# Agent attention and a top-1 expert layer on one core: the agents' scale in four parts, first queries and next keys at other steps, stores and transposes asked for later

## The chip, the cores and the metric

The kernel runs on one core of one Trainium2 chip. A time is device microseconds (us) of one execution of the whole program. The kernel before has a median of 1130.12 us over three runs (1129.23 to 1131.7). The engines are called as the profile calls them: PE is the matrix engine (PEld its weight loads), DVE the vector engine, ACT the scalar engine, POOL the general one, SP the engine that issues most transfers.

## The reference

Four batches of 11,456 tokens with 128 channels pass through attention by way of 49 agents, and the result through a layer of 8 experts of which each token uses the best one.

```python
scale = 1 / sqrt(128)
def sm(a, b):                       # softmax of scale * a b^T over the last axis
    ...
a2k = sm(agents, k)                 # (4, 49, 11456)
agent_v = a2k @ v                   # (4, 49, 128)
x = (sm(q, agents) @ agent_v).reshape(45824, 128)
logits = x @ w_gate                 # 8 experts
expert_idx = argmax(logits)
gate_w = softmax(logits)[expert_idx]
for e in range(8):
    xe = x[expert_idx == e]
    out[expert_idx == e] = gate_w * (relu(xe @ w1[e]) @ w2[e])
```

The inputs q, k and agents are drawn with a standard deviation of 0.8, v with 0.1.

## The kernel before

**Tiling.** A batch is cut into 11 chunks of 1024 tokens and one of 192. A chunk of keys or queries is loaded (`load`, L306), its scale is found (squares on ACT, L359; the power of two from bits of the sum on DVE and POOL, L230 to L237), and it is split into two float16 parts, high by ACT (L393) and low by DVE (L395), in the tile `hl`. A transfer that transposes (`turn_over`, L421) writes `hT`, in which the channels lie on the partitions; there are two buffers of it for keys and two for queries. Scores against the agents are three matmuls for each 128 tokens (`scores`, L462 to L464). From scores of keys come exponentials S and their two parts `eh`: ACT L537 and L562, POOL L556 (a running sum `es`) and L564. They are multiplied with the values (`values`, L594, accumulated by DVE L603). From scores of queries come exponentials E and `mm`, which a transfer transposes to `M` (L716).

**The loop.** The product of attention with the chosen expert's first matrix is folded into 49 rows `Ah`, `Al`, so a batch's main loop is 23 groups of 512 tokens times 8 slices of 128 hidden channels, 184 steps. A step is layer 1 of its slice (PE L1300 and L1301 into `ph`, of which there are four), relu and splitting (ACT L1306, DVE L1307 into `hh`), and layer 2 of the slice five steps back (12 matmuls, L1321). Each batch uses one expert in the loop (the commonest); tokens that chose another are gathered behind all four loops and done in blocks. Step 7 of batch 1 is written b1:7 here. By layer 1's first matmul, b0:0 starts 71.9 us into the profiled execution, b1:0 at 340.4, b2:0 at 593.0, b3:0 at 832.7, and the last step at 1069.9.

**What sets the order.** All other work is laid between the steps by a table of numbers. `at(t, f)` puts a piece of work f at step t, counted over all four batches, on a heap; `after(dt, f)` puts it dt steps behind the piece that is running. The pieces are issued in order of t. On each engine the program order is that of the issue, and the engine keeps to it, whatever is ready. SP's own order is kept too (`issue_after(queue[-1])`). In `attention`, KS and KT are the step of a batch's first keys, counted from the batch's own step 0, and the steps between chunks; QA, QB and QC the same for queries. A later batch's keys and values, and its first queries, therefore lie in the loops ahead of its own: KS = -211 is step 157 of the batch two ahead; the agents' scale (`agent_squares`, `agent_split`) stands three and two steps ahead of the first keys, so that of batch 2 at b0:154 and that of batch 3 at b1:154. DTR, DTE, DEX and DST are how many steps behind its producer a transfer or an addition is put: the transposes of `hl` to `hT` (DTR), the transposes of mm (DTE), the store of exponentials (DEX), and the stores of the output (DST). For the first batch everything ahead of step 0 is a prologue with numbers of its own (KS0 and so on).

Of the kernel before, what the change touches and what calls it, by code (L numbers as in the profile page):

```python
# [12 lines left out]
F32 = mybir.dt.float32  # L13
# [3 lines left out]
AF = mybir.ActivationFunctionType  # L17
# [4 lines left out]
P = 128  # L22
A = 49
# [22 lines left out]
KS0, KT0, KL0, VT0, VL0, QS0, QT0, QL0 = -200, 2, 4, 2, 1, -172, 3, 2.5  # L46
VE, T1, TF0, TF1, TL, TLM, Q0 = 12, 1.75, 3, 1.5, 18, 10, 2

KS, KT, VT, VL, VL4, TW0, TW1, DW = -211, 9, 5.3, 8, 5, 8, 2.5, 1
QA, QB, QC, QB3, KL, LL, UD, RG, D1, DL = -23, 8, 13, 10.5, 12, 9.5, 2, 0.7, 0.5, 0  # L50

KS1 = []

# [2 lines left out]

SLA, SLD, SLP = 2, 2, 1.5

DTR, DTE, DEX, DST, DXS = 3.5, 2, 3, 3, 0.5
TE0, TE1 = 5, 6.5  # L60

LAG = 5

# [13 lines left out]
def agent_moe_kernel(ctx, tc, q, k, v, agents, wg, w1, w2, out):  # L77
    nc = tc.nc
    B, N, D = q.shape
    E = wg.shape[1]  # L80
# [24 lines left out]
    ranks = nc.dram_tensor("ranks", (PAIRS * P, R), F32).ap()  # L105
    avd = nc.dram_tensor("avd", (B, A, D), F32).ap()
# [7 lines left out]
    ones = cpool.tile([P, P], F32, name="ones")  # L114
# [51 lines left out]
    two = pl("two", 2)  # L166
# [7 lines left out]
    def small_ps():  # L174
        return psS.tile([P, 512], F32, tag="s", name="ps_small")
# [100 lines left out]
    def at(t, f, *a):  # L276
        count[0] += 1
        heapq.heappush(events, (t, count[0], f, a))

    def after(dt, f, *a):  # L280
        at(now[0] + dt, f, *a)
# [7 lines left out]
    def attention(b):  # L289
        st = state[b]  # L290
        base = b * steps
# [19 lines left out]
        AG = {}  # L311

        def agent_squares():
            for x in range(b, min(b + 2, B)):
                if x not in agents_in:
                    agents_in[x] = two.tile([P, D], F32, tag="ag", name="ag")
                    nc.sync.dma_start(agents_in[x][:A], agents[x])
            ag = AG["ag"] = agents_in[b]
            nc.vector.tensor_scalar(ag[:A], ag[:A], scale, None, op0=ALU.mult)
            jk = one.tile([P, CH], F16, tag="jk", name="jk")  # L320
            sa = two.tile([P, 1], F32, tag="sa", name="sa")
            nc.vector.memset(sa, 0.0)
            nc.scalar.activation(jk[:A, :D], ag[:A], AF.Square, accum_out=sa[:A])
            pt = small_ps()
            nc.tensor.matmul(pt[:, :1], ones, sa, start=True, stop=True)
            sab = two.tile([P, 1], F32, tag="sab", name="sab")
            nc.vector.tensor_copy(sab, pt[:, :1])
            AG["mul"], div = scale_bits(sab, P, 1, "as")

            AG["bits"] = two.tile([P, 1], F32, tag="bits", name="bits")  # L330
            nc.vector.tensor_scalar(AG["bits"], div[:, :1].bitcast(I32), float((50 - 127) * (1 << 23)), None, op0=ALU.add)
# [273 lines left out]
        def agentvalues(i):  # L605
# [6 lines left out]
            elif i == 1:  # L612
                pt = small_ps()
# [5 lines left out]
            elif i == 2:  # L619
# [4 lines left out]
                if first:  # L624
                    pt = small_ps()
# [9 lines left out]
            elif i == 3:  # L635
# [8 lines left out]
                pt = small_ps()  # L644
                nc.tensor.transpose(pt[:, :P], AV["av"], ident)
                ava = one.tile([A, D], F32, tag="ava", name="ava")
                nc.vector.tensor_copy(ava, pt[:A, :P])
                nc.sync.dma_start(avd[b], ava)
            else:
                G = AV["G"]  # L650
                gpw, ginv = pow2_scale(AV["gm"], 1)
# [214 lines left out]
        ks, kt, kl, vt, vl = (KS0, KT0, KL0, VT0, VL0) if first else (KS, KT, KL, VT, VL)  # L866
        dl = 0 if first else DL
        ka = KS1[0] - base if b == 1 and KS1 else ks
        at(base + ka - 3, agent_squares)
        at(base + ka - 2, agent_split)  # L870
        for c in range(NCK):
            t = KS1[c] - base if b == 1 and c < len(KS1) else ks + kt * c
            use(t, "k", c)
# [57 lines left out]
    def leftover_ranks(b):  # L931
# [3 lines left out]
        C = one.tile([P, E, R], F32, tag="cum", name="C")  # L935
# [20 lines left out]
        pt = small_ps()  # L956
# [1 line left out]
        nc.tensor.matmul(pt[:, E:2 * E], ones, cp[:, NCK, :], start=True, stop=True)  # L958
        nc.vector.tensor_copy(C[:, :, NT], pt[:, :E])
        nc.vector.tensor_tensor(ends_[:, b * E:(b + 1) * E], pt[:, :E], cp[:, NCK, :], op=ALU.add)  # L960
        nc.sync.dma_start(ranks[b * E * P:(b + 1) * E * P, :].rearrange("(e p) c -> p e c", p=P), C)

        nbi = one.tile([P, E], I32, tag="nbi", name="nbi")
        nc.vector.tensor_scalar(nbi, pt[:, E:2 * E], float(P - 1), None, op0=ALU.add)
# [416 lines left out]
    for j in range(2 * E):  # L1381
        b, i = divmod(j, -(-2 * E // (B - 1)))
# [14 lines left out]
    while events:  # L1397
# [3 lines left out]
        with ExitStack() as held:  # L1401
            if now[0] > 0 and queue:
                held.enter_context(tc.issue_after(queue[-1]))
            if not (f is next and a[0] in steps_of):
                for x, s in ((1, SLP), (2, SLA), (3, SLD)):
                    p = next((p for p in reversed(paced) if p[0] <= now[0] - s), None)
# [76 lines left out]
```

## Time and profile before

| what | value |
|---|---|
| median of 3 runs | 1130.12 us |
| the profiled execution | 1129.85 us, of which the span is 1128.1 us |
| PE busy | 1021.4 us, 91% of the span |
| DVE busy | 1000.8 us, 89% |
| ACT busy | 829.3 us, 74% |
| POOL busy | 214.5 us, 19% |
| mean granted clock of PE | 0.969 |

The span runs from the first instruction to the last; 1.75 us of the profiled execution lie outside it. A busy share says how long an engine had an instruction in work. The granted clock is what the throttle gave to PE, 1.00 being 2.4 GHz and 0.50 being 1.2 GHz. In a timeline, the square brackets at the end of a row hold the engine's idle time ahead of the row and what ended it.

### The profile page before, as it was taken

What the parts mean: (1) busy time and instruction counts of PE and PEld (TensorE: products, weight loads), DVE (VectorE), ACT (ScalarE), POOL (GpSimd) and SP (SyncE); (2) the same over time, 40 slices, a digit from 0 to 9 for tenths busy, and PEclk for the clock granted to TensorE, in tenths of its full rate; (3) what the DMA queues carried; (4) which work ended last, traced back from release to release, by engine and by line L of the source; (5) the groups of instructions that cost most, each with busy time, mean ns of one, the idle gap of its engine ahead of it and who ended that gap; (6) DMA issues with size and microseconds to landing.
All of it is one profiled execution on the core that took longest, in us unless ns stands there. A gap on an engine that the chain in (4) does not pass through costs nothing. (4 is left out here: it accounts for less than half of the span.)

```text
span 1128.1 us, 35718 instructions
## 1 busy us (share of the span) xinstructions
PE 1021.4 (91%) x14575; PEld 823.6 (73%) x14575; DVE 1000.8 (89%) x2372; ACT 829.3 (74%) x1495; POOL 214.5 (19%) x369
## 2 busy tenths in 40 slices
PE   7847999989899999999889999999999988989995
PEld 7725877777776778777667778777777766767795
DVE  5876998999888998998788998998899998799894
ACT  6556887888787887888677887888677665656681
POOL 1300000134400011233300011234200113110133
PEclk9866999999999999999899999999999999999998
DMA  8579789633399998645299998634467653433470
GB/s 324 182 231 211 196 179 206 168 107 119 108 268 205 212 209 204 158 127 182 84 241 223 198 214 204 170 114 159 119 177 167 148 112 84 133 102 125 119 249 14
DMA packets 263592, 190.49 MB, mean 169 GB/s; under 512 B 215433, under 2 KB 228226, under 8 KB 263424
## 3 DMA queue, kind: packets, MB, share of 16 engines
q1 hardware_dynamic: 261856, 185.92, 64.0%
q0 software_dynamic: 1568, 2.25, 1.0%
q8 instruction: 115, 1.88, 0.7%
q14 instruction: 53, 0.43, 0.1%
HBM read 99.75 MB, written 36.43 MB: 121 GB/s over the span
## 5 line engine op out<-in xcount | busy, mean ns | idle before, releaser
L1321 PEld LDWEIGHTS <-hh 128*128 128x128 f16 x8640 | 550.4, 99 | 168.7 <-issue 8.9
L1321 PE MATMUL py<-w2h,hh 128*128 128x128 f16 (+1 forms) x5760 | 609.8, 220 | 1.1 <-issue 0.9
L1321 PE MATMUL py<-w2l,hh 128*128 128x128 f16 (+1 forms) x2880 | 526.5, 220 | 1.2 <-issue 1.2
L1306 ACT ACTIVATE hh<-ph 128x512 f16<-128x512 f32 (+1 forms) x728 | 407.8, 581 | 146.6 <-PE ph L1301 139.1
L1307 DVE SCALAR_TENSOR_TENSOR hh<-ph,hh 128x512 f16<-128x512 f32 (+1 forms) x736 | 478.2, 665 | 29.4 <-ACT hh L1306 26.6
L1300 PE MATMUL ph<-M,Ah 128*128 128x512 f16 (+1 forms) x736 | 276.7, 376 | 35.3 <-DVE hh L1307 23.6
L1301 PE MATMUL ph<-M,Al 128*128 128x512 f16 (+1 forms) x736 | 276.7, 376 | 0.2 <-DVE Al L814 0.2
L395 DVE SCALAR_TENSOR_TENSOR hl<-ld,mul,hl 128x1024 f16<-128x1024 f32 (+1 forms) x119 | 148.5, 1255 | 14.6 <-ACT hl L393 12.0
L393 ACT ACTIVATE hl<-ld,mul 128x1024 f16<-128x1024 f32 (+1 forms) x119 | 128.7, 1091 | 29.9 <-DVE mul L234 26.8
L359 ACT ACTIVATE jk<-ld 128x1024 f16<-128x1024 f32 (+1 forms) x126 | 126.2, 1001 | 5.2 <-DMA ld<-in_k_dram 3.9
L237 POOL TENSOR_SCALAR div<-hb,bits 128x1 int32<-128x1 int32 (+1 forms) x90 | 27.0, 300 | 470.3 <-DVE hb L230 443.9
L1301 PEld LDWEIGHTS <-Al 128*128 128x128 f16 x736 | 71.8, 98 | 36.0 <-issue 33.8
L1300 PEld LDWEIGHTS <-Ah 128*128 128x128 f16 x736 | 73.5, 100 | 9.3 <-DMA M<-mm 4.9
L462 PEld LDWEIGHTS <-hT 128*128 128x128 f16 (+1 forms) x622 | 52.7, 99 | 23.5 <-DMA hT<-hl 22.8
L462 PE MATMUL ps_s<-agh,hT 128*128 128x49 f16 x558 | 52.6, 186 | 13.8 <-DMA hT<-hl 12.0
L1334 DVE TENSOR_TENSOR yo<-py,cs 128x512 f32<-128x512 f32 (+1 forms) x92 | 61.5, 669 | 2.9 <-PE py L1321 2.8
L463 PEld LDWEIGHTS <-hT 128*128 128x128 f16 (+1 forms) x622 | 51.6, 99 | 3.2 <-issue 2.9
L464 PE MATMUL ps_s<-agh,hT 128*128 128x49 f16 x558 | 52.3, 186 | 0.0
L463 PE MATMUL ps_s<-agl,hT 128*128 128x49 f16 x558 | 52.3, 186 | 0.0
L464 PEld LDWEIGHTS <-hT 128*128 128x128 f16 (+1 forms) x622 | 51.3, 98 | 0.0
L556 POOL TENSOR_TENSOR es<-es,S 128x392 f32<-128x392 f32 (+1 forms) x33 | 33.4, 1011 | 92.8 <-ACT S L537 76.1
L699 ACT ACTIVATE E<-E,ln,div 128x392 f32<-128x392 f32 (+1 forms) x47 | 32.4, 689 | 14.1 <-DVE E L693 13.2
(319 smaller groups left out, 1344.6 us busy)
## 6 DMA issues: line engine op xcount, KB each, us to landing
ld<-in_k_dram SPq DMA_DIRECT2D x44, 512.0 KB
ld<-in_v_dram SPq DMA_DIRECT2D x44, 512.0 KB
ld<-in_q_dram SPq DMA_DIRECT2D x44, 512.0 KB
out_dram<-yo SPq DMA_DIRECT2D x88, 256.0 KB
w1e<-in_moe_w_dram SPq DMA_DIRECT2D x18, 512.0 KB
w2e<-in_moe_w_dram SPq DMA_DIRECT2D x18, 512.0 KB
exps<-E SPq DMA_DIRECT2D x44, 196.0 KB
wn<-in_moe_w_dram SPq DMA_DIRECT2D x16, 512.0 KB
```

The costliest lines, as they stand in the source:

```text
L359: nc.scalar.activation(jk[:p, :t * D], x[:p, :t, :].rearrange("p t d -> p (t d)"), AF.Square, accum_out=ss[:p])
L393: nc.scalar.activation(hi[:p, :t, :], x[:p, :t, :], AF.Copy, scale=m)
L395: nc.vector.scalar_tensor_tensor(lo[:p, :t, :], x[:p, :t, :], m, hi[:p, :t, :], op0=ALU.mult, op1=ALU.subtract)
L462: nc.tensor.matmul(o, x[:, 0, i, :p], AG["h"], start=True, stop=False)
L463: nc.tensor.matmul(o, x[:, 0, i, :p], AG["l"], start=False, stop=False)
L464: nc.tensor.matmul(o, x[:, 1, i, :p], AG["h"], start=False, stop=True)
L1300: x1 = nc.tensor.matmul(ph[:, :nn], st['Ah'][:, f, :], m, start=True, stop=False)
L1301: nc.tensor.matmul(ph[:, :nn], st['Al'][:, f, :], m, start=False, stop=True)
L1306: x2 = nc.scalar.activation(hh[:, 0, :nn], ph[:, :nn], AF.Relu)
L1307: x3 = nc.vector.scalar_tensor_tensor(hh[:, 1, :nn], ph[:, :nn], 0.0, hh[:, 0, :nn], op0=ALU.max, op1=ALU.subtract)
L1321: mm_ = lambda l, r, **k: nc.tensor.matmul(o, l, r, skip_group_check=True, **k)
L1334: nc.vector.tensor_tensor(yo[:p, :n, :], py[:p, :n * D].rearrange("p (i d) -> p i d", d=D), cs.unsqueeze(2).broadcast_to([p, n, D]), op=AL ...
```

## The change

Five things are changed, all in when a piece of work is asked for; nothing that is computed changes.

- **Agents' scale.** `agent_squares` is cut into three: the loads of the agents with DVE's scaling and clearing (`agent_squares`), ACT's sum of squares (`agent_sums`), and PE's sum over the partitions with the bits (`agent_scale`). With `agent_split` they stand 9, 7, 5 and 2.5 steps ahead of the first keys, where `agent_squares` stood 3 and `agent_split` 2 ahead.
- **Keys.** KS goes from -211 to -207 and KT from 9 to 8.6: the first keys of a later batch come 4 steps later, the last 0.4 earlier.
- **Queries.** QA goes from -23 to -27 and QB from 8 to 11: the first three chunks at steps -27, -16 and -5 where they were at -23, -15 and -7; later chunks 2 steps later (for the last batch as well). For batch 0 chunks 1 and 2 go from -15 and -7 to -16 and -5.
- **Transfers.** DTR 3.5 to 4.5, DTE 2 to 3, DEX 3 to 6, DST 3 to 5; the small stores `avd` and `ranks` 5 steps later (DAV).
- **Agents' values.** The pieces of `agentvalues` for later batches stand 6 and 8 steps behind the last keys' exponentials, before 5 and 6.5.

```diff
-KS, KT, VT, VL, VL4, TW0, TW1, DW = -211, 9, 5.3, 8, 5, 8, 2.5, 1
-QA, QB, QC, QB3, KL, LL, UD, RG, D1, DL = -23, 8, 13, 10.5, 12, 9.5, 2, 0.7, 0.5, 0
+KS, KT, VT, VL, VL4, TW0, TW1, DW = -207, 8.6, 5.3, 8, 5, 8, 2.5, 1
+QA, QB, QC, QB3, KL, LL, UD, RG, D1, DL = -27, 11, 13, 10.5, 12, 9.5, 2, 0.7, 0.5, 0
...
-DTR, DTE, DEX, DST, DXS = 3.5, 2, 3, 3, 0.5
-TE0, TE1 = 5, 6.5
+DTR, DTE, DEX, DST, DXS = 4.5, 3, 6, 5, 0.5
+TE0, TE1, DAV = 6, 8, 5
+AG0, AG1, AG2, AG3 = 9, 7, 5, 2.5
...
             nc.vector.tensor_scalar(ag[:A], ag[:A], scale, None, op0=ALU.mult)
+            AG["sa"] = two.tile([P, 1], F32, tag="sa", name="sa")
+            nc.vector.memset(AG["sa"], 0.0)
+
+        def agent_sums():
             jk = one.tile([P, CH], F16, tag="jk", name="jk")
-            sa = two.tile([P, 1], F32, tag="sa", name="sa")
-            nc.vector.memset(sa, 0.0)
-            nc.scalar.activation(jk[:A, :D], ag[:A], AF.Square, accum_out=sa[:A])
+            nc.scalar.activation(jk[:A, :D], AG["ag"][:A], AF.Square, accum_out=AG["sa"][:A])
+
+        def agent_scale():
             pt = small_ps()
-            nc.tensor.matmul(pt[:, :1], ones, sa, start=True, stop=True)
+            nc.tensor.matmul(pt[:, :1], ones, AG["sa"], start=True, stop=True)
...
-                nc.sync.dma_start(avd[b], ava)
+                after(DAV, nc.sync.dma_start, avd[b], ava)
...
-        at(base + ka - 3, agent_squares)
-        at(base + ka - 2, agent_split)
+        for x, f in ((AG0, agent_squares), (AG1, agent_sums), (AG2, agent_scale), (AG3, agent_split)):
+            at(base + ka - x, f)
...
-        nc.sync.dma_start(ranks[b * E * P:(b + 1) * E * P, :].rearrange("(e p) c -> p e c", p=P), C)
+        after(DAV, nc.sync.dma_start, ranks[b * E * P:(b + 1) * E * P, :].rearrange("(e p) c -> p e c", p=P), C)
```

The line numbers of the changed kernel are higher by 5 from the agents' functions on (L1300 is L1305 there, L1307 is L1312). Three places where the order of the instructions differs:

**PE, steps 154 to 156 of batch 1.** This is the order before: the sum over the agents' squares (L325) and that of the keys' exponentials (L615) stand ahead of layer 1 of step 155, the last product with the values (L594, `eh`) behind that of step 156.

```order
L325 MATMUL ps_small<-sa,ones 128x1
L615 MATMUL ps_small<-e_11104,ones 128x49
L1300 LDWEIGHTS Ah
L1300 MATMUL ph<-M,Ah 128x512
L1301 LDWEIGHTS Al
L1301 MATMUL ph<-M,Al 128x512
...
L335 MATMUL ps_small<-ident,ag 128x49
```

And this is the order now, from layer 1 of step 155 on:

```order
L1305 MATMUL ph<-M,Ah 128x512
...
L599 MATMUL ps_s<-eh,hl 128x49
L620 MATMUL ps_small<-e_11106,ones 128x49
L1305 LDWEIGHTS Ah
L1305 MATMUL ph<-M,Ah 128x512
L1306 LDWEIGHTS Al
L1306 MATMUL ph<-M,Al 128x512
...
L330 MATMUL ps_small<-sa,ones 128x1
```

The agents' sum has moved from ahead of step 155 to behind layer 1 of step 156, and the product with the values from behind step 156 to ahead of it.

**DVE, between the low parts of steps 1 and 2 of batch 0.** L1307 is a step's low part of `hh`; L505, L691, L693 and L706 are pieces of the keys' and queries' softmax; L395 is the low part of a chunk. Before, from the first score of keys on to the low part of step 2:

```order
L497 COPY mx<-S 128x392
L230 TENSOR_SCALAR hb<-ss 128x1
L234 TENSOR_SCALAR mul<-hb 128x1
L505 TENSOR_TENSOR mx<-mx,S 128x392
L691 TENSOR_REDUCE mq<-ps_y 128x8
L230 TENSOR_SCALAR hb<-ss 128x1
L693 TENSOR_TENSOR E<-ps_y,mq 128x392
L234 TENSOR_SCALAR mul<-hb 128x1
L395 SCALAR_TENSOR_TENSOR hl<-ld,mul,hl 128x1024
L706 CAST mm_144<-E 128x8x49
L1307 SCALAR_TENSOR_TENSOR hh<-ph,hh 128x512
```

The same stretch now:

```order
L502 COPY mx<-S 128x392
L696 TENSOR_REDUCE mq<-ps_s 128x8
L231 TENSOR_SCALAR hb<-ss 128x1
L1312 SCALAR_TENSOR_TENSOR hh<-ph,hh 128x512
L698 TENSOR_TENSOR E<-ps_s,mq 128x392
```

Seven instructions that stood ahead of step 2's low part now stand behind it. On PE the score matmuls between layer 1 of steps 5 and 6 go from four groups of eight to three, and the groups that followed steps 6, 12 and 13 follow steps 7, 14 and 15.

**SP, ahead of the transposes of batch 2's first `M`.** Before, from the two transposes of chunks ahead of it:

```order
L421 DMA_TRANSPOSE hT<-hl 128x16x128 x2
L306 DMA ld<-in_k_dram 128x1024
L1409 DMA out_dram<-yo 128x512
L1409 DMA exps<-E 128x392
L306 DMA ld<-in_q_dram 128x1024
L716 DMA_TRANSPOSE M<-mm_143 128x8x128
```

Now, from the same two transposes on:

```order
L426 DMA_TRANSPOSE hT<-hl 128x16x128 x2
L1414 DMA exps<-E 128x392
L721 DMA_TRANSPOSE M<-mm_143 128x8x128
L1414 DMA out_dram<-yo 128x512
L307 DMA ld<-in_k_dram 128x1024
L307 DMA ld<-in_q_dram 128x1024
```

The store of the output and both loads have moved from ahead of `M` to behind it. It is the same ahead of batch 1's.

## Rows read from the trace of the kernel before

**Rows 1.** Page, part 1: busy time, share of the span, instructions.

```profile
PE 1021.4 (91%) x14575; PEld 823.6 (73%) x14575; DVE 1000.8 (89%) x2372; ACT 829.3 (74%) x1495; POOL 214.5 (19%) x369
```

**Rows 2.** Timeline of PE, two undisturbed steps of batch 0: start, length, instruction.

```profile
100.25 0.38 PE L1300 MATMUL ph<-M,Ah 128*128 128x512 f16 x1
101.35 0.38 PE L1300 MATMUL ph<-M,Ah 128*128 128x512 f16 x1
```

**Rows 3.** Stretches: start:end, length, busy by engine (instructions), clock, DMA share, GB/s.

```profile
77.80:98.20 20.40, 10.30 (x149) 8.18 (x149) 13.75 (x26) 14.67 (x23) 2.04 (x5) 0.50 1.07 202
...
320.10:323.50 3.40, 3.40 (x34) 2.85 (x31) 2.37 (x11) 2.60 (x4) 0.00 (x0) 0.50 1.23 194
...
545.40:552.20 6.80, 6.10 (x40) 4.54 (x41) 3.82 (x15) 4.15 (x9) 0.74 (x4) 0.50 0.00 0
...
593.20:596.60 3.40, 3.40 (x26) 2.50 (x25) 1.45 (x4) 1.72 (x3) 0.00 (x0) 0.50 1.29 249
```

**Rows 4.** Timeline of PE, batch 0 from step 5 on.

```profile
81.02 0.59 PE L1300 MATMUL ph<-M,Ah 128*128 128x512 f16 x1 [4.55 <-DVE mul L234]
...
92.45 0.22 PE L462 MATMUL ps_y<-agh,hT 128*128 128x49 f16 x1 [2.73 <-DMA hT<-hl]
...
94.71 0.63 PE L1300 MATMUL ph<-M,Ah 128*128 128x512 f16 x1
```

**Rows 5.** Timeline of DVE, the same stretch.

```profile
89.76 0.57 DVE L691 TENSOR_REDUCE mq<-ps_y 128x8 f32<-128x392 f32 x1 [0.48 <-PE ps_y L464]
...
92.37 0.68 DVE L1307 SCALAR_TENSOR_TENSOR hh<-ph,hh 128x512 f16<-128x512 f32 x1
```

**Rows 6.** Timeline of PE at step 155, batches 1 and 2.

```profile
546.10 0.59 PE L325 MATMUL ps_small<-sa,ones 128*128 128x1 f32 x2 [3.72 <-ACT jk L323]
...
796.65 0.42 PE L615 MATMUL ps_small<-e,ones 128*128 128x49 f32 x2 [1.65 <-DVE e L610]
```

**Rows 7.** Timeline of DVE ahead of it, batch 1.

```profile
543.14 0.81 DVE L610 TENSOR_REDUCE e<-es 128x49 f32<-128x392 f32 x1 [1.98 <-POOL es L556]
...
545.49 0.06 DVE L322 MEMSET sa<- 128x1 f32 x1
```

**Rows 8.** Timeline of POOL, the same stretch.

```profile
540.30 2.46 POOL L949 TENSOR_TENSOR cp<-cp,C 128x8 f32<-128x8 f32 x9
542.72 0.39 POOL L556 TENSOR_TENSOR es<-es,S 96x98 f32<-96x98 f32 x1
...
543.50 0.37 POOL L564 TENSOR_TENSOR eh<-S,eh 96x98 f16<-96x98 f32 x1
```

**Rows 9.** Timeline of PE, batch 0, step 151.

```profile
293.57 0.74 PE L594 MATMUL ps_s<-eh,hl 128*128 128x49 f16 x23 [1.87 <-POOL eh L564]
```

**Rows 10.** Timeline of PE, batches 0 and 1, step 170.

```profile
319.60 0.20 PE L462 MATMUL ps_s<-agh,hT 128*128 128x49 f16 x1 [1.90 <-DMA hT<-hl]
...
572.26 0.20 PE L462 MATMUL ps_s<-agh,hT 128*128 128x49 f16 x1 [3.05 <-DMA hT<-hl]
```

**Rows 11.** Timeline of SP, its transfers ahead of b1:170 and of b2:0.

```profile
562.05 5.74 SPq L421 DMA_TRANSPOSE hT<-hl  x1
...
576.39 7.84 SPq L421 DMA_TRANSPOSE hT<-hl  x2
584.28 0.58 SPq L306 DMA_DIRECT2D ld<-in_k_dram  x1
...
586.76 1.52 SPq L716 DMA_TRANSPOSE M<-mm  x1
```

**Rows 12.** Stretches of batch 1, columns as in rows 3.

```profile
550.00:556.00 6.00, 6.00 (x68) 4.67 (x67) 4.18 (x14) 3.41 (x6) 0.28 (x1) 0.82 0.01 3
...
560.00:566.00 6.00, 6.00 (x73) 4.78 (x72) 5.42 (x19) 4.74 (x8) 0.39 (x2) 1.00 0.81 253
...
587.00:590.00 3.00, 3.00 (x67) 3.00 (x65) 2.91 (x9) 2.64 (x6) 0.21 (x1) 1.00 1.04 391
```

**Rows 13.** Timeline of PE's weight loads at b2:0.

```profile
592.99 0.10 PEld L1300 LDWEIGHTS <-Ah 128*128 128x128 f16 x1 [2.45 <-DMA M<-mm]
```

## The prediction, made before the changed kernel ran

> **What bounds the kernel now.** I read the page's busy shares first. PE works 91% of the span and DVE 89% [rows 1], so nothing is idle for long, and a gain can only come from the places where PE stands. The second view was the timeline of PE over some undisturbed steps: layer 1 starts every 1.10 us [rows 2], and 4 x 184 such steps are 810 us of the 998 between the first and the last. The rest is attention's matmuls, and waits. The third view, PE's timeline with its idle times, gives the waits, and the fourth, the stretches, gives what comes behind them: behind a long wait the granted clock falls to 0.50, that is 1.2 GHz, for 3.4 us or a multiple, while PE is busy through nearly all of it [rows 3]. Where PE sets the pace, 3.4 us at half the clock cost 1.7 us, and 6.8 cost 3.4. So a wait has two prices, and both are in the sum below. In the loops the waits of some size are few: the start of batch 0 [rows 4], step 155 of batches 1 and 2 [rows 6], b0:151 [rows 9], step 170 of batches 0 and 1 [rows 10], and the first steps of batches 1 and 2 [rows 13] (one of the two stands there; the other is at 340.36 us, with 2.33 us on PE). I cost the change at these, since each is a place where an order written by the table lets PE arrive ahead of its input.
>
> **The change part by part.** The sum is made against the profiled execution's own 1129.85 us, 0.27 under the median of the three runs, which is less than their spread.
>
> *The agents' scale, b1:154.* PE waits 3.72 us at 546.10 for ACT's squares [rows 6]. Behind that stands a chain: POOL's `es` begins at 542.72, behind nine small additions that take 2.46 us [rows 8]; DVE's L610 waits for it and begins at 543.14; only behind L610, and two low parts, does DVE clear `sa` at 545.49 [rows 7], and ACT and PE follow. Now DVE's two instructions are asked for at b1:150, ahead of L610, and PE's sum at step 156. The wait for the squares goes. What is late next is the product with the last values, L594, now ahead of step 156: PE would come to it at about 546.10 - 3.72 + 1.10 = 543.48, and POOL's `eh` ends at 543.87 [rows 8], with ten of the additions ahead of it where there were eleven. That leaves 0.1 to 0.4 us. With the clock's 6.8 us at half [rows 3] the term is -3.72 + 0.4 - 3.4 = -6.7 us. If L594 waits long enough for the clock to fall all the same, only some 2 us are won: -7.1 to -2.
>
> *The same place in batch 2.* No agents are prepared there, but PE waits 1.65 us for L610 [rows 6], which waits for the same POOL instruction. Three additions stand ahead of it now instead of nine: six times 0.273 us (2.46 / 9) is 1.6 us. Term -1.65, bounds -1.65 and 0.
>
> *Batch 0, step 151.* POOL's order is unchanged there, but the product with the values, which waits 1.87 us for `eh` [rows 9], has moved one step ahead on PE. PE arrives 1.10 us earlier and waits 2.97. Whether the clock falls is open: it did not behind these 1.87 us, and did behind 1.90 at 319.60 [rows 3, 10]. So +1.1 or +2.8; I take the middle, +2.0.
>
> The Trainium skill, TensorE: Matmul & The Clock Gate, Part 1, says that the span over which activity is judged runs free of the program, so that the same matmuls meet a different number of slow ones from run to run. The 1.87 and 1.90 us, one without and one with a slow stretch, agree. By it this term is drawn anew, 1.1 or 2.8, and so is that of every wait of nearly two microseconds that stays; the sum would be one time 1.7 us higher or lower, which the range holds.
>
> *Step 170 of batches 0 and 1.* PE waits 1.90 and 3.05 us for a transposed chunk [rows 10]. SP is held in order by the choice of the expert, the transfers stand nearly still until then (3 GB/s at 550 to 556), and then come two weight loads, a chunk's load and the transposes, asked for at 562.05 [rows 11, 12]. In the changed order the transposes (now of queries) still stand behind two weight loads and a chunk, and behind a store of 256 KB which used to be gone before; at 253 GB/s [rows 12] that is 1.0 us, twice: +2.0. The small store `avd` now stands behind the transposes. Bounds: 0, and +4 if the clock stays low for one stretch more.
>
> *The first steps of batches 1 and 2.* At b2:0 PE's weight load waits 2.45 us for the transposed `M` [rows 13], and a half-clock stretch of 3.4 us follows [rows 3]. `M` is asked for at 586.76, behind the chunk loads, a store and 0.2 MB of exponentials which follow the transposes of 576.39 to 584.23 [rows 11]. Now it stands behind those transposes and the exponentials alone. From the choice of the expert on, two chunk loads of 0.52 MB fewer lie ahead of it; at the 391 GB/s that the queue moved from 587 to 590 [rows 12] 1.05 MB are 2.7 us, at 253 GB/s 4.1. PE itself comes 1.0 us later by the term before. 2.7 + 1.0 against 2.45 leaves a margin of 1.25 us; the wait goes, twice with its stretch: 2 x (2.3 + 1.7) = -8.0. Bounds -8 and 0. The margin is the smallest of the sum's.
>
> *The start.* Between layer 1 of steps 5 and 6 PE has four groups of score matmuls, each behind its own transposes; it is done with the third at 92.45 - 2.73 = 89.72, waits 2.73 us for the fourth, and issues layer 1 of step 6 at 94.71 [rows 4]. Step 6 also needs DVE's low part of step 2, which comes at 92.37, behind seven other pieces, one of them the maximum L691 at 89.76 [rows 5]. In the changed order three groups stand ahead of step 6, and the low part directly behind L691, so it would be done by 89.76 + 0.57 + 0.68 = 91.0, and step 6 can begin there: 3.7 us earlier. If the queries' transposes land earlier, as the order of scores suggests, it is 89.7 and 5.0 us. I take -4. The fourth wait is then covered by steps 6 and 7. Bounds: -7, if one slow stretch of those from 77.8 to 98.2 [rows 3] ends sooner, and +1, if the groups now behind steps 7, 14 and 15 wait as they did.
>
> *All else*: keys 8.6 steps apart, later queries, the later additions, stores and transposes. Most of it only moves work over steps with little idle time. The batch whose queries come first at b2:169, where they came at 173, can show a wait as in batches 0 and 1: at most 3.05 + 1.7 = 4.7 us. Other pieces may fall better or worse by a low part of DVE or two (0.68 us). I take +2, bounds -2 and +5; the later stores are hidden as long as PE never waits for their buffers, which no wait of before names.
>
> *Sum*: -6.7 - 1.65 + 2.0 + 2.0 - 8.0 - 4 + 2 = -14.35, so 1115.5 us.
>
> **The rivals.** *The boundaries stay* (1123.5 us). The margin of 1.25 us is not there, because the transposes ahead of `M` take the queue longer; SP needed 7.84 us to issue two of them [rows 11], which speaks for it. Against it stands that the bytes taken away are worth more than the wait by either rate. Then 8 us of the sum are missing: -6.4.
>
> *The waits come back elsewhere* (1128.2). As the boundaries' rival, and batch 2 gets the wait of 4.7 us at step 169 in full where I took 2, and the start wins 2 instead of 4: -6.4 + 2.7 + 2 = -1.7. For it speaks that the transfers are still released by the choice of the expert, and that a wait for them is what PE shows at each such place now [rows 10, 13]. Against it, that batch 2 has less ahead of its transposes than the two others: the ranks and a chunk's load now stand behind them.
>
> *The transposes are late throughout* (1135.5): the case that ends slower. An addition of one step is put ahead of every transpose of a loop, while its scores stay as many steps behind the request; every transposed chunk has 1.10 us less. The place is the crowded end of each batch, where four of them lie behind loads, three batches long: twelve waits of 1.1 us, four of them with a slow stretch of 1.7, are 20 us, and -14.35 + 20 is +5.6. It decides from the point where a chunk's slack in the old order is under 1.1 us. For it: the first of each four was late already [rows 10]. Against it: the other three of each four show no wait of note in the old order, though SP needs up to 5.74 us to issue one [rows 11].
>
> **How the numbers follow.** The forecast gets 0.58, the boundaries' rival 0.20, the waits that come back 0.10, the late transposes 0.12. A measurement of this kernel can tell about 0.2%, or 2.3 us, from no change; the first two cases are faster by more (0.78), the third lies within (0.10), the fourth is slower (0.12). The bounds of the terms, all at their good ends, give -25, at their bad ends +11; few of them will be together. The range goes from 1107 to 1130: below it lie about 0.05, above it the late transposes and a little more.
>
> **What would show it.** Layer 1 of b1:155 should follow that of 154 within 1.6 us, at a clock of 1.00; the squares of the agents should release nothing on PE. At b1:0 and b2:0 no weight load should wait for `M` over 0.5 us, and the clock should stay up there. At step 170 of batches 0 and 1 the wait should still be there, at 2 to 4 us, and at b0:150 one near 3 us for POOL. Layer 1 of b0:6 should follow that of b0:5 by some 10 us, where it is 94.71 - 81.02 = 13.69 now. I am wrong if a wait over 2 us stands at b1:0 or b2:0 (then 1123 or more), or if waits for transposed chunks appear at the second to fourth chunk of a batch's end.

## The result, and the profile after

The changed kernel takes 1115.56 us, the median of four runs (1113.33 to 1116.81), where the kernel before takes 1129.67, the median of four as well, three of them those named at the start: a ratio of 0.9877, interval 0.9857 to 0.9897. The forecast was 1115.5. The total is right, and of its terms only some: two came out near their size, the start came out larger and the boundaries smaller by some 3 us each, and what had been taken together as "all else" holds a loss of 7.5 us and a gain of 5.5. The total also hangs on the chip: on another one the same kernel is 0.47% faster than before. Three executions of the experiments lie far outside the others of their kernels (1279, 2888.5 and 3501.46 us), and the times and ratios of changed kernels below are without them.

The table puts the two traces side by side, by the start of layer 1 (the first matmul of a step) in each. A minus says that the changed kernel needs less for the stretch.

| stretch | forecast, us | measured, us |
|---|---|---|
| up to b0:0 | 0 | -0.5 |
| b0:0 to b0:16, the start | -4 | -6.8 |
| b0:16 to b0:88 | 0 | +7.5 |
| b0:88 to b0:144 | 0 | -1.9 |
| b0:144 to b0:160 | +2.0 | +1.5 |
| b0:160 to b1:16, and b1:160 to b2:16 (step 170 and the boundary) | +2.0 - 8.0 | -1.3 and -2.1 |
| b1:152 to b1:160, the agents | -6.7 | -6.3 |
| b2:144 to b2:160 | -1.65 | -0.7 |
| b3:40 to b3:104 | 0 | -5.5 |
| all else | +2 | +1.6 |

The page's first part after, one row (columns as in [rows 1]):

```profile
PE 1012.3 (91%) x14575; PEld 817.4 (73%) x14575; DVE 995.0 (89%) x2372; ACT 830.2 (75%) x1495; POOL 214.6 (19%) x369
```

Of the last row of the table 2.1 us lie behind the last step; that part takes 57.4 to 60.4 us in the traces of all the kernels here. PE has lost 9 us of busy time with the same instructions, and the other engines next to nothing; the shares are the old ones.

The timeline of PE after, at the places of [rows 4], [rows 6], [rows 9], [rows 10] and [rows 13], and at new ones: three in batch 0 (b0:25, b0:50 and b0:76) and b2:7:

```profile
80.52 0.59 PE L1305 MATMUL ph<-M,Ah 128*128 128x512 f16 x1 [0.38 <-DVE mul L235]
...
88.16 0.63 PE L1305 MATMUL ph<-M,Ah 128*128 128x512 f16 x1
...
119.00 0.20 PE L467 MATMUL ps_s<-agh,hT 128*128 128x49 f16 x1 [1.96 <-DMA hT<-hl]
...
152.08 0.20 PE L467 MATMUL ps_s<-agh,hT 128*128 128x49 f16 x1 [1.68 <-DMA hT<-hl]
...
187.98 0.20 PE L467 MATMUL ps_s<-agh,hT 128*128 128x49 f16 x1 [2.68 <-DMA hT<-hl]
...
282.10 0.57 PE L1305 MATMUL ph<-M,Ah 128*128 128x512 f16 x1 [2.63 <-DVE hh L1312]
...
292.15 0.74 PE L599 MATMUL ps_s<-eh,hl 128*128 128x49 f16 x23 [1.09 <-POOL eh L569]
...
319.52 0.20 PE L467 MATMUL ps_s<-agh,hT 128*128 128x49 f16 x1 [2.79 <-DMA hT<-hl]
...
339.64 0.38 PE L1305 MATMUL ph<-M,Ah 128*128 128x512 f16 x1 [1.49 <-DVE hh L1312]
...
542.54 0.28 PE L599 MATMUL ps_s<-eh,hl 96*128 96x49 f16 x5 [0.44 <-POOL eh L569]
...
564.04 0.20 PE L467 MATMUL ps_s<-agh,hT 128*128 128x49 f16 x1 [3.16 <-DMA hT<-hl]
...
584.25 0.38 PE L1305 MATMUL ph<-M,Ah 128*128 128x512 f16 x1 [1.49 <-DVE hh L1312]
...
592.57 0.20 PE L467 MATMUL ps_s<-agh,hT 128*128 128x49 f16 x1 [1.49 <-DMA hT<-hl]
```

Read from the top: layer 1 of b0:6 follows that of b0:5 by 7.64 us (13.69 before); three waits for transposed chunks have come up later in batch 0; at b0:151 the wait for POOL has become shorter, but one for DVE six steps earlier has grown from 1.45 to 2.63; step 170 waits 0.9 and 0.1 us longer than before; the first steps of batches 1 and 2 no longer wait for M but for DVE, 1.49 us, and a transposed chunk is waited for at b2:7; and at b1:156 the 3.72 us have become 0.44.

The stretches of the changed kernel behind those waits, and one in batch 0 (columns as in [rows 3]):

```profile
180.00:182.00 2.00, 2.00 (x29) 1.63 (x27) 2.00 (x4) 1.19 (x2) 0.00 (x0) 1.00 0.00 0
...
282.10:285.50 3.40, 3.40 (x39) 2.67 (x39) 3.03 (x7) 1.85 (x4) 3.06 (x7) 0.51 0.36 139
319.70:323.10 3.40, 3.40 (x42) 2.85 (x39) 2.46 (x8) 0.28 (x2) 0.00 (x0) 0.50 1.15 281
...
542.00:548.80 6.80, 6.36 (x81) 5.02 (x79) 6.80 (x22) 5.56 (x9) 2.94 (x8) 1.00 0.03 13
565.40:568.80 3.40, 3.40 (x21) 2.28 (x19) 3.40 (x15) 1.20 (x2) 0.28 (x1) 0.51 1.22 207
584.30:587.70 3.40, 3.33 (x39) 2.36 (x39) 3.09 (x9) 2.82 (x6) 0.52 (x1) 1.00 1.21 161
```

The slow clock behind the agents and at the two boundaries is gone. It is still there behind step 170, and a new stretch stands behind the DVE wait at 282.10. The first row is the other thing to see: some us ahead of the wait at 187.98 the transfers stand quite still, 0 GB/s.

DVE ahead of b1:0 in the changed kernel, where L1312 at 339.24 is the low part of b0:180, for which layer 1 of b1:0 waits:

```profile
335.04 0.69 DVE L1339 TENSOR_TENSOR yo<-py,cs 128x512 f32<-128x512 f32 x1
335.65 1.28 DVE L859 SCALAR_TENSOR_TENSOR w2l<-w2e,mul,w2h 128x1024 f16<-128x1024 f32 x1
336.85 2.48 DVE L400 SCALAR_TENSOR_TENSOR hl<-ld,mul,hl 128x1024 f16<-128x1024 f32 x2
339.24 0.35 DVE L1312 SCALAR_TENSOR_TENSOR hh<-ph,hh 128x192 f16<-128x192 f32 x1
```

An output scaling, the split of the expert's second matrix and the low parts of two chunks, 4.2 us, lie ahead of a low part of 0.35 us, at the place in the batch where steps are shortest (192 tokens). Before, the low part of b0:180 had one chunk ahead of it, and the split behind it:

```profile
336.15 1.28 DVE L395 SCALAR_TENSOR_TENSOR hl<-ld,mul,hl 128x1024 f16<-128x1024 f32 x1
337.36 0.15 DVE L847 SCALAR_TENSOR_TENSOR kk<-ppw,div 128x1 f32<-128x1 f32 x1
337.42 0.35 DVE L1307 SCALAR_TENSOR_TENSOR hh<-ph,hh 128x192 f16<-128x192 f32 x1
337.69 1.27 DVE L854 SCALAR_TENSOR_TENSOR w2l<-w2e,mul,w2h 128x1024 f16<-128x1024 f32 x1
```

It was done at 337.77, 0.26 us ahead of PE, which came at 338.03 (340.36 less its wait of 2.33) and waited for M. So this pile is one that the change itself makes.

### The profile page after: what moved, and what is told of

Read it like the earlier page. It is cut to its first block, busy times and chain, and to the rows that moved or that the text cites. A ratio compares the mean times of both kernels' runs of the same rounds, so it can differ in the third digit from the quotient of the medians.

```text
span 1113.8 us, 35704 instructions
## 1 busy us (share of the span) xinstructions
PE 1012.3 (91%) x14575; PEld 817.4 (73%) x14575; DVE 995.0 (89%) x2372; ACT 830.2 (75%) x1495; POOL 214.6 (19%) x369
## 5 line engine op out<-in xcount | busy, mean ns | idle before, releaser
L1312 DVE SCALAR_TENSOR_TENSOR hh<-ph,hh 128x512 f16<-128x512 f32 (+1 forms) x736 | 477.0, 665 | 23.0 <-ACT hh L1311 21.6
L1305 PE MATMUL ph<-M,Ah 128*128 128x512 f16 (+1 forms) x736 | 276.0, 375 | 29.7 <-DVE hh L1312 26.6
L400 DVE SCALAR_TENSOR_TENSOR hl<-ld,mul,hl 128x1024 f16<-128x1024 f32 (+1 forms) x119 | 145.6, 1230 | 17.1 <-ACT hl L398 16.2
L1305 PEld LDWEIGHTS <-Ah 128*128 128x128 f16 x736 | 73.3, 100 | 3.2 <-issue 1.7
L467 PE MATMUL ps_s<-agh,hT 128*128 128x49 f16 x574 | 53.7, 186 | 20.8 <-DMA hT<-hl 18.2
L467 PEld LDWEIGHTS <-hT 128*128 128x128 f16 (+1 forms) x622 | 51.5, 98 | 22.3 <-DMA hT<-hl 22.1
L469 PE MATMUL ps_s<-agh,hT 128*128 128x49 f16 x574 | 53.5, 186 | 0.0
L468 PEld LDWEIGHTS <-hT 128*128 128x128 f16 (+1 forms) x622 | 50.6, 98 | 3.4 <-issue 3.1
L469 PEld LDWEIGHTS <-hT 128*128 128x128 f16 (+1 forms) x622 | 50.4, 98 | 0.0
L542 ACT ACTIVATE S<-S,ln 128x392 f32<-128x392 f32 (+1 forms) x48 | 28.2, 599 | 21.8 <-DVE S L537 16.5
```

The costliest lines, as they stand in the source:

```text
L400: nc.vector.scalar_tensor_tensor(lo[:p, :t, :], x[:p, :t, :], m, hi[:p, :t, :], op0=ALU.mult, op1=ALU.subtract)
L467: nc.tensor.matmul(o, x[:, 0, i, :p], AG["h"], start=True, stop=False)
L468: nc.tensor.matmul(o, x[:, 0, i, :p], AG["l"], start=False, stop=False)
L469: nc.tensor.matmul(o, x[:, 1, i, :p], AG["h"], start=False, stop=True)
L1305: x1 = nc.tensor.matmul(ph[:, :nn], st['Ah'][:, f, :], m, start=True, stop=False)
L1312: x3 = nc.vector.scalar_tensor_tensor(hh[:, 1, :nn], ph[:, :nn], 0.0, hh[:, 0, :nn], op0=ALU.max, op1=ALU.subtract)
```

## The experiments

Each is a few numbers of the table, in the changed kernel or in the one before. Times are medians; ratios are to the kernel before on the same chip. Four kernels each shared a chip, so that kernels of different groups are compared by their ratios and by stretches of their traces.

### What gave the start's gain back

In the changed kernel, one step of delay ahead of the chunks' transposes is taken back:

```diff
-DTR, DTE, DEX, DST, DXS = 4.5, 3, 6, 5, 0.5
+DTR, DTE, DEX, DST, DXS = 3.5, 3, 6, 5, 0.5
```

> The changed kernel with the transposes of chunks asked for as early as before (DTR 3.5 again, all else as changed). Theory A: the addition of one step is what gives the start's gain back, because in batch 0 the transposes stand unasked for while the transfers idle; the waits for a transposed chunk at b0:25 (1.96 us), b0:50 (1.68) and b0:76 (2.68) fall under 0.5 us each, steps 24 to 88 of batch 0 get 4 to 6 us shorter, and the time is 1109 to 1112 us. Theory B: the addition pays elsewhere (the order of the transfers at the ends of batches 0 and 1), so the boundaries lose what batch 0 wins: 1114 to 1117. Theory C: those waits come from the keys' new spacing, not from the addition; they stay, and the time is 1115.5.

Measured: 1112.02 us, ratio 0.9857 (0.9804 to 0.991); this interval overlaps that of the changed kernel, and what the step is worth is read from the stretches. The three waits of batch 0 are gone, b0:16 to b0:88 is 6.8 us shorter than in the changed kernel, and the wait came up again in another place, that of theory B in kind but not in place. The two rows of PE, b1:56 and b2:7:

```profile
403.72 0.38 PE L730 MATMUL ps_s<-Gs,M 128*128 128x18 f16 x8 [2.90 <-DMA M<-mm]
...
585.32 0.20 PE L467 MATMUL ps_s<-agh,hT 128*128 128x49 f16 x1 [2.55 <-DMA hT<-hl]
```

So theory A holds for batch 0: the transposes were held back there while the transfers idled. With chunks' transposes earlier and M's not, M is now behind them in SP's order, and logits at b1:56 and b2:56 wait for it, with a slow clock behind: 3.7 to 3.8 us in each batch. Taking back the addition ahead of M's transposes as well:

```diff
-DTR, DTE, DEX, DST, DXS = 4.5, 3, 6, 5, 0.5
+DTR, DTE, DEX, DST, DXS = 3.5, 2, 6, 5, 0.5
```

> The changed kernel with both additions ahead of transposes taken back (DTR 3.5, DTE 2). With DTR alone taken back, batch 0 won 7.6 us, and logits at b1:56 and b2:56 then waited 2.9 and 2.0 us for M, which is asked for behind the chunks' transposes now. Theory A: M asked for one step (1.1 us) earlier gets ahead of them again; those waits fall under 1 us, the slow clock behind them goes, 1105 to 1109. Theory B: the transfers are full there and M only changes places with a chunk; the waits move to score matmuls, 1111 to 1114.

Measured: 1116.38 us, ratio 0.9877 (0.9855 to 0.9898). By its trace theory A is right, and the total does not show it: beside the kernel with DTR alone, steps 40 to 72 of batch 1 are 3.8 us shorter and steps 48 to 64 of batch 2 3.1, and logits wait 0.45 us at most for M; but steps 40 to 104 of batch 3 are 9.2 us longer, where nothing was changed. What this is stands under batch 3 below. There the kernel was run again beside the changed one.

### The agents

The kernel before, with the four parts alone:

```diff
-        at(base + ka - 3, agent_squares)
-        at(base + ka - 2, agent_split)
+        for x, f in ((9, agent_squares), (7, agent_sums), (5, agent_scale), (2.5, agent_split)):
+            at(base + ka - x, f)
```

> The kernel before with the agents' scale in four parts 9, 7, 5 and 2.5 steps ahead of the keys, and nothing else of the change. Theory A: the split alone takes away the chain at b1:155, but the sum of the keys' exponentials now waits there for the slow additions of the general engine, as in batch 2 (1.65 us): -3.72 + 1.6 - 3.4 = -5.5, so about 1124.3 us. Theory B: the gain at b1:155 came from the new order on the general engine, which this kernel does not have: the 3.7 us wait stays under another name with its slow clock, 1128 to 1130.

Measured: 1129.64 us, ratio 1.0013 (0.9992 to 1.0035): nothing. PE at b1:155, then DVE and POOL ahead of it:

```profile
548.39 0.26 PE L340 MATMUL ps_small<-ident,ag 49*128 49x49 f32 x1 [3.66 <-DVE acc L608]
```

```profile
547.35 0.81 DVE L615 TENSOR_REDUCE e<-es 128x49 f32<-128x392 f32 x1 [3.84 <-POOL es L561]
548.08 0.26 DVE L608 SCALAR_TENSOR_TENSOR acc<-ps_s,div,acc 128x49 f32<-128x49 f32 x1
```

```profile
542.06 3.30 POOL L954 TENSOR_TENSOR cp<-cp,C 128x8 f32<-128x8 f32 x12
545.32 1.47 POOL L956 TENSOR_TENSOR C<-C,cp 128x704 f32<-128x704 f32 x1
546.75 0.22 POOL L958 TENSOR_TENSOR C<-C,cp 128x16 f32<-128x16 f32 x1
546.92 0.40 POOL L561 TENSOR_TENSOR es<-es,S 96x98 f32<-96x98 f32 x1
```

The wait is as long as in [rows 6], with another name on it. PE's next matmul into a small buffer (here the agents' transpose) needs one that DVE's L608 must read first, L608 stands behind L615, and L615 waits for POOL's sum as in [rows 7]. The number is theory B's. But the run does not test the split alone, since POOL's order in batch 1 is not that of before: the sum `es` stood behind nine of the small additions [rows 8] and stands behind all twelve and two more here. It ends at 547.32, 2.6 us after PE has come (548.39 - 3.66 = 544.73); before, it ended 0.7 us after (543.11 and 542.38), and the other 3.0 of the 3.72 us were the way from there over DVE and ACT to the squares. So POOL begins the chain in both, the squares were most of the wait before, and what the split takes off at the squares POOL's later sum puts on again. What the split would win with POOL's old order was not run. The opposite test is the changed kernel with the scale in one piece again:

```diff
-AG0, AG1, AG2, AG3 = 9, 7, 5, 2.5
+AG0, AG1, AG2, AG3 = 3, 3, 3, 2
```

> The changed kernel with the agents' scale in one piece again, 3 steps ahead of the first keys, and the split 2 ahead; all else as changed. Theory A, after the split alone gained nothing: the keys' later start puts the agents behind the products with the values, so the four parts are worth nothing; steps 152 to 168 of batch 1 stay within 1 us and the time at 1114 to 1117. Theory B: the split and the new place are needed together; a wait of 2 to 4 us for the squares comes back near b1:159, with a slow clock behind it, 1119 to 1122.

Measured: 1126.56 us, ratio 0.9964 (0.995 to 0.9978), 11 us more than the changed kernel had taken, and it reads like theory B. The trace says A: steps 152 to 168 of batch 1 differ by 0.3 us from the changed kernel's, the wait at b1:156 is the same 0.44 us for POOL, and PE comes to the squares at b1:160 without a wait. The traces differ by 8.5 us at the end, and 8.8 of that (the rest cancels) come up in steps 40 to 104 of batch 3, in which no agents are prepared. So the four parts were out as the cause, and batch 3 was open. The keys' numbers alone, in the kernel before:

```diff
-KS, KT, VT, VL, VL4, TW0, TW1, DW = -211, 9, 5.3, 8, 5, 8, 2.5, 1
+KS, KT, VT, VL, VL4, TW0, TW1, DW = -207, 8.6, 5.3, 8, 5, 8, 2.5, 1
```

> The kernel before with the keys' numbers alone (first keys 4 steps later, 8.6 apart). Theory A: the keys carry most of the change: at the start three groups of scores stand ahead of layer 1 of b0:6 instead of four, -3 to -7; at b1:155 the general engine's sum stands behind seven additions instead of nine and the agents' squares come only at b1:160, so of the 3.72 us some 1 to 1.5 stay and the slow clock goes, -4 to -6: 1118 to 1122. Theory B: the start's gain is given back by the later waits for chunks as in the changed kernel, leaving -4 to -6: 1123 to 1126. Theory C: the keys are worth nothing without the other parts: 1128 to 1130.

Measured: 1120.93 us, the median of three, ratio 0.9906 (0.9878 to 0.9934), theory A. The start wins 8.0 us and keeps them, since the transposes are not delayed; b1:152 to b1:168 wins 5.0. The waits of PE that are left at b1:154 and b1:160, and that of its weight load at b2:0:

```profile
538.82 0.42 PE L615 MATMUL ps_small<-e,ones 128*128 128x49 f32 x2 [0.31 <-DVE e L610]
...
546.43 0.38 PE L325 MATMUL ps_small<-sa,ones 128*128 128x1 f32 x2 [0.80 <-ACT jk L323]
```

```profile
584.87 0.10 PEld L1300 LDWEIGHTS <-Ah 128*128 128x128 f16 x1 [3.87 <-DMA M<-mm]
```

The 3.72 us have become 0.31 for POOL's chain and 0.80 for the squares, without the split. POOL's sum stands behind seven additions here, behind nine before and behind three in the changed kernel. At the boundaries PE waits longer for M, 3.87 us where 2.45 were [rows 13]: part of what the keys win is lost there.

### The boundaries

The queries' numbers alone, in the kernel before:

```diff
-QA, QB, QC, QB3, KL, LL, UD, RG, D1, DL = -23, 8, 13, 10.5, 12, 9.5, 2, 0.7, 0.5, 0
+QA, QB, QC, QB3, KL, LL, UD, RG, D1, DL = -27, 11, 13, 10.5, 12, 9.5, 2, 0.7, 0.5, 0
```

> The kernel before with the queries' numbers alone (first three chunks at steps -27, -16 and -5, the later ones 2 steps later). Theory A: M is ready for b1:0 and b2:0, but DVE's pile ahead of the low part of step 180 stays, so that each boundary wins 1 to 1.6 us; batch 3 wins another 1 to 2: 1124.5 to 1127. Theory B: boundaries win all that was forecast for them, 8: 1119 to 1122. Theory C: nothing, since the later stores are what put M ahead in the order of transfers: 1128 to 1130.

Measured: 1131.35 us, ratio 1.0009 (0.9992 to 1.0026): theory C's number and not its reason. Its trace is 2.4 us ahead of that of before at b3:40, and 4.7 us are lost in steps 40 to 104 of batch 3, of which below. At the boundaries M is in time (b1:0 and b2:0 wait 1.02 and 1.15 us, for DVE), and the chunks' transposes behind it are late instead, two steps on:

```profile
342.42 0.22 PE L462 MATMUL ps_s<-agh,hT 128*128 128x49 f16 x1 [3.75 <-DMA hT<-hl]
```

Next, whether DVE's pile is a matter of its place. In the changed kernel the split of the expert's second matrix (L859) goes 7.5 steps later:

```diff
-WO = (0, 2.5, 5, 9.5, 11, 12.5)
+WO = (0, 2.5, 5, 9.5, 11, 20)
```

> The changed kernel with the split of the expert's second matrix 7.5 steps later, at b1:1 and b1:2, so that 1.28 us less of DVE lie ahead of the low part of b0:180, for which layer 1 of b1:0 waits 1.49 us now. Theory A: DVE's pile of work just there has taken the place of the transfer of M; each of the two waits falls to 0.2 to 0.5 us and the time by about 2, to 1113.5. Theory B: DVE's load over the whole stretch is the bound, so the wait only moves by some steps: 1115.5 within 1. Theory C: M lands hardly earlier than before, and the first steps wait for it again, 1115 to 1117, with M named at the weight load.

Measured: 1122.2 us, the median of four, ratio 0.9935 (0.991 to 0.9959), 6.6 us more than the changed kernel. The 1.49 us at b1:0 and b2:0 are gone, and M is not waited for, so that C is out; at b1:7 PE and its weight load wait:

```profile
350.80 0.10 PEld L467 LDWEIGHTS <-hT 128*128 128x128 f16 x1 [1.78 <-DMA hT<-hl]
350.80 0.20 PE L467 MATMUL ps_s<-agh,hT 128*128 128x49 f16 x1 [1.67 <-DVE Ld L748]
```

DVE and the transposed chunk end this wait within 0.1 us of each other, so the row does not say which of the two set it; the low parts of the chunks to be transposed run at 340.46 here and at 336.85 in the changed kernel, so DVE's later work delays the transposes too. The wait has moved on, as theory B said, and it costs more than that: b0:176 to b1:8 is 2.3 us longer than in the changed kernel, b2:0 to b2:32 1.5. Of the 7.3 us between the spans of the two traces 4.5 lie ahead of b0:80, where the order is the same: the waits for chunks there differ that much between two executions. Last, the stores as early as before:

```diff
-DTR, DTE, DEX, DST, DXS = 4.5, 3, 6, 5, 0.5
-TE0, TE1, DAV = 6, 8, 5
+DTR, DTE, DEX, DST, DXS = 4.5, 3, 3, 3, 0.5
+TE0, TE1, DAV = 6, 8, 0
```

> The changed kernel with the stores asked for as early as before (DEX 3, DST 3, DAV 0). Theory A: M still stands directly behind the same two transposes, so the boundaries keep what they won, and the stores ahead of chunk transposes cost batch 0 up to 2 us: 1115 to 1118 on a chip where the changed kernel takes 1115.5. Theory B: the later stores are what frees the transfers at the ends of the batches; the waits for M return, 4 to 8 us more.

Measured: 1130.85 us, where the changed kernel takes 1125.45 on the same chip (ratios 1.0012, 0.9991 to 1.0032, and 0.9953, 0.9935 to 0.9971). The later stores are worth 5 us in the medians, theory B's size, but no wait for M came back: the waits are for chunks, at b1:9 (2.72 us), b2:8 and b2:9 (1.05 and 1.72) and b2:172 (2.46). The two profiled executions are less than 1 us apart in span (that of the changed kernel is its longest of eleven), so that the traces can't tell where the 5 us lie; these waits are what speaks for a place.

### Batch 3

In the changed kernel, the last batch's later queries two steps earlier, as they were:

```diff
-                     QA + 2 * QB + (QB3 if last else QC) * (c - 2))
+                     QA + 2 * QB - (2 if last else 0) + (QB3 if last else QC) * (c - 2))
```

> The changed kernel with the last batch's fourth and later chunks of queries two steps earlier, which is where they stood before. Theory A: the 6.4 us that batch 3 gained come from these two steps, which part the queries from the gathers that lie at fixed steps: steps 40 to 100 of batch 3 lose 4 to 6.5 us again, 1120 to 1122. Theory B: they come from the later stores and transposes, and the time stays within 1 us of 1115.5.

Measured: 1118.35 us, ratio 0.9901 (0.9871 to 0.9931). Steps 40 to 104 of batch 3 take 87.1 us, 85.7 in the changed kernel: the two steps are worth 1.4 us there, not 5.5. The same stretch takes 91.2 in the kernel before, and 87.8 in the kernel with the four parts alone, whose order in batch 3 is that of before. So 3.4 us of the 5.5 are no matter of order. That the last kernels all took 91 to 96 us there, on one chip, made the chip itself suspect. So the changed kernel was run once more, and so was the one with the agents in one piece:

> The changed kernel, unaltered, beside the one with the agents' scale in one piece. The traces so far fall in two kinds by the time that steps 40 to 104 of batch 3 take: 85 to 88 us in five of them, 91 to 96 us in the five others, in which the matrix engine idles there with nothing that the profile names. The kinds may go by kernel or by chip (the four last kernels, all of the slow kind, ran on one chip). Theory A, by kernel: here it is 85.7 us again, the time 1115 to 1117, and the one-piece kernel stays 9 us slower. Theory B, by chip: on a chip of the slow kind this kernel too shows 92 to 96 us and some 1122 to 1126, on one of the other kind both show 85 to 87.

> The kernel with the agents' scale in one piece again, the rest as changed, on the same chip as the changed kernel. Theory A (the slow kind goes by kernel): 1124 to 1127 with 94 us in steps 40 to 104 of batch 3. Theory B (by chip): within 2 us of the changed kernel on this chip, so that the four parts are worth nothing.

Measured: 1125.45 us (ratio 0.9953, 0.9935 to 0.9971) and 1127.55 (0.9972, 0.9954 to 0.9989). Theory B: it goes by chip, and the kernel with the agents in one piece is 2.1 us slower, with intervals that overlap, so that the four parts are not shown to be worth anything. Steps 40 to 104 of batch 3 as one stretch, first the changed kernel in the first trace, then the same kernel on the other chip:

```profile
868.18:953.90 85.72, 80.11 (x1107) 63.29 (x1105) 80.42 (x206) 56.93 (x116) 19.14 (x22) 1.00 0.56 132
```

```profile
872.84:967.51 94.67, 82.98 (x1107) 63.66 (x1105) 80.82 (x206) 56.27 (x116) 18.41 (x22) 1.00 0.50 120
```

The same 1107 matmuls at the same clock take 9 us more. 8.4 of it lie at four places, b3:50, 60, 82 and 91, where POOL gathers rows by indirect transfers. Steps 80 and 81 on the other chip, PE's rows that waited for nothing the profile names, and POOL's:

```profile
934.62 0.22 PE L1326 MATMUL py<-w2l,hh 128*128 128x128 f16 x1 [0.47 <-issue]
...
935.37 0.27 PE L1326 MATMUL py<-w2h,hh 128*128 128x128 f16 x2 [0.36 <-issue]
```

```profile
931.72 1.01 POOL L243 DMA_INDIRECT fg<-ranks,fri  x1 [0.30 <-issue]
933.04 1.01 POOL L243 DMA_INDIRECT fg<-ranks,fri  x1 [0.30 <-issue]
934.36 1.01 POOL L243 DMA_INDIRECT fg<-ranks,fri  x1 [0.30 <-issue]
```

PE goes on by two or four matmuls at a time, with 0.4 us between, while these run. In the first trace the same gathers stand at 922.42, 923.74 and 925.05, and PE shows no such row. The kernel before shows six such rows in its trace, but loses 3.4 us there (91.2 against the 87.8 above), the changed one 9. On the chips of this kind the order of before takes 91.2 us over these steps and the order with the later queries 94.3 to 96.2, on the first kind 87.8 and 85.7: the sign of what the later queries do there depends on the chip. So the chip has a large part in what this change is worth: 14.1 us in the first comparison, 5.5 in this one. By the medians the kernel before differs by 1.8 us between the chip of the first four kernels and this one (1129.12 and 1130.95). On which chip the first comparison ran, and whether both kernels' traces came from one, is not known. Last, the transposes as early as before on that chip:

> The kernel with both additions ahead of transposes taken back (DTR 3.5, DTE 2), on the same chip as the changed kernel. Its earlier trace was 3.6 us shorter than the changed kernel's up to b3:0 and beyond, and 9 us longer in steps 40 to 104 of batch 3. If that goes by chip, it is 5 to 9 us faster than the changed kernel here; if by kernel, the two are within 2 us.

Measured: 1115.84 us, ratio 0.9875 (0.9849 to 0.99), 9.6 us less than the changed kernel beside it, a little more than the first of the two cases said. (The 3.6 us of the expectation are misread: its earlier trace was 7.4 us ahead of the changed kernel's at b3:0.) By the traces b0:16 to b0:88 is 8.9 us shorter, and no wait for a transfer of a chunk over 0.9 us is left between b0:16 and b0:170. This version beats both kernels on the chip on which all three were run.

## Why the prediction was right, and where it was not

**The agents' term** was right in size (-6.3 for -6.7) and only in part in cause. The step that failed is "The wait for the squares goes" as the work of the four parts: the split alone won nothing, and taking it out of the changed kernel costs 0.3 us at its place, while the keys' numbers alone won 5.0 of the 6.9 us of steps 152 to 168. They put fewer of POOL's additions ahead of its sum and the agents behind the values. The chain of [rows 6 to 8] was read rightly, and it begins at POOL; that the split alone moves POOL's sum back was not seen. What was forecast to be late next, L594 by 0.1 to 0.4 us, is what is late, by 0.44.

**Batch 2's wait** of 1.65 us went as forecast. The stretch won 0.7 all the same, since two waits for DVE there (b2:145 and b2:150) grew by 0.6 and 0.75.

**The boundaries** were forecast at -8 with step 170 at +2. Together they gave -3.4. M is in time, as the term said, with its slow clock gone; what was missed is what comes next: DVE, 1.49 us, at each boundary, and the transposed chunk at b2:7, also 1.49, a wait of the kind that "What would show it" names as a sign of being wrong. The term worked out its margin from the transfers alone and did not look at DVE's new order there, which puts two chunks and the split ahead of the low part of b0:180. Moving the split by 7.5 steps took the 1.49 us away and made the wait at b1:7 1.67 us, from 0.52; that DVE's load over the boundary is the bound, and not its order, is likely by that and not shown. None of the rivals had DVE.

**The start** won 6.8 for 4, near the end of its bounds: step 6 follows at 7.64 us, not 10. And it was given back. "All else" was taken at +2, as work moved "over steps with little idle time", and the delay ahead of the transposes cost 7 us in batch 0. The rival of late transposes had this mechanism, and placed it at the crowded ends of the batches. It struck where the transfers stood idle, since there the delay is not hidden behind anything.

**Batch 3** was forecast at nothing and gave 5.5 us: 1.4 by the queries' two later steps, 3.4 without a change of order, by the chip as far as the other runs show, 0.7 not explained.

**b0:151**: the wait for POOL became 1.09 us and did not grow to 2.97, since 2.63 us for DVE at b0:145, 1.45 before, come first. Both numbers come with the keys' spacing: 2.62 and 1.09 with the keys' numbers alone, 1.47 and 1.96 with the split alone. The two waits together have grown by 0.4 us, and a slow stretch stands behind the first; that this is near the forecast (+1.5 for +2.0) is luck. For the clock, the rule that the prediction takes from the Trainium skill (TensorE: Matmul & The Clock Gate, Part 1) did better than my reading of the rows. Behind waits of 1.96 and 2.68 us in batch 0 no slow stretch came, behind 2.63 and 2.79 one did. On the other chip the wait of 2.78 us at 189.04, which is the 2.68 here, had one. The length of a wait alone does not say it.

So errors of -2.8 us at the start, +7.5 behind it, +2.6 at the boundaries and -5.5 in batch 3 nearly cancelled. That the total came out within 0.1 us is luck: a forecast that hits the total shows little of its terms.

## What to carry to other kernels

When a wait has one name on it, follow its chain to the engine that is late before crediting an edit that moves the last link: here the last link was moved and another took its place at the same length. When one part of a change is run alone, read every engine's order again: the split alone had moved POOL's sum, so that its run does not say what the split is worth. When a transfer is taken off a path, look at every engine at that place for who is next, not only at the queue; and delay a transfer only where the queue is full, since where it stands idle each step of delay is a step of waiting. Run a kernel on a second chip before a gain of one per cent is called its own.

## What was not expected of the hardware

- On the two chips of the last eight kernels every trace shows PE's matmuls coming in pieces of two or four with 0.4 us between while POOL's indirect gathers run: 9 us in the changed kernel's batch 3, with the same instructions at the same clock. On the chip of the first four, and in the changed kernel's first trace, none does. The profile names no releaser, and nothing here tests what the cause is.
- The same order of instructions differs by up to 3.8 us over the first 80 steps of batch 0 between executions, all of it in waits for transposed chunks and in the slow clock behind them. A single trace of that stretch bears no conclusion under 4 us.
